# DeltaNet and a GELU block: copies of the queries' scores split over two engines, weight conversions placed later in a slot, one DMA moved to another queue

## The chip, the cores and the metric

The kernel runs on one core of a Trainium2 chip. The core has five engines with instruction queues of their own: PE (TensorE, matrix products), DVE (VectorE), ACT (ScalarE), POOL (GpSimd) and SP (SyncE), which here only issues DMAs. Each engine works through its queue in order; semaphores tie the queues together. The metric is the time of one execution in device microseconds; lower is better.

## What is computed

Four sequences (B) with eight heads (H), 768 tokens (S) and a head size of 48 (D) run through a recurrence with a delta rule; its output, laid out as 3072 rows of 384, runs through two dense layers with a quick GELU between them.

```python
k_n = k / (np.linalg.norm(k, axis=-1, keepdims=True) + 1e-06)
for t in range(S):
    y[:, :, t] = np.einsum('bhd,bhde->bhe', q[:, :, t], state)
    v_old = np.einsum('bhde,bhd->bhe', state, kt)
    state = state + bt[:, :, :, None] * np.einsum('bhd,bhe->bhde', kt, vt - v_old)
...
h = x @ w_in                             # 3072 x 384 by 384 x 2048
g = h * (1.0 / (1.0 + np.exp(-1.702 * h)))
return (g @ w_out).astype(np.float32)    # 2048 x 384
```

The attention inputs are float32. The weights w_in and w_out arrive as float64, so the kernel has to turn them into float32 itself.

## The kernel before

**Units.** The sequence is cut into 6 chunks of 128 tokens (C); a unit n is one chunk of one sequence with all its heads, 24 units, chunk by chunk (units 0 to 3 are chunk 0). Inside a chunk the recurrence is a triangular system in four blocks of 32 rows.

**Keys.** `prepare(n)` transposes the normalized keys (kT), multiplies them with themselves (psG), copies the products from PSUM to G (two copies; from unit 10 on the second is DVE's) and sends G to memory (Nd), from where the 32 x 32 diagonal blocks come back as NT with (head, block) on the partitions. `invert` inverts these blocks on DVE, for all four sequences at once in chunk 0 and for two at a time later (names NT, P, YB, YS); YS goes out to memory (Yd) and comes back as XB. In `prepare` both transfers of G are issued by SP: line 377 (Nd) and line 383 (NT).

**A unit's step.** `scores` transposes the queries (psT to QS) and forms their products with the keys (psQ); in chunks after the first the same product also holds a correction for V, which DVE subtracts at line 526. Line 527 copies the scores out of PSUM to M, four copies per unit, all on ACT; POOL then masks M (line 530). The substitution goes through the blocks 0 to 3: `solve` multiplies XB with V into psU, `solved` copies it to US on ACT, `below` multiplies G with it into psR, and `rest` subtracts psR from V on DVE. `outputs` gives psY, copied to xT and last; six small DMAs per pair of units move a part of last into xT (line 615).

**The dense layers.** `hidden` multiplies xT with w_in (ph, line 631) and applies the GELU on ACT (gT, line 636), `written` multiplies gT with w_out (po, line 646). They are generators; what is ready stands in `queue`.

**Weights.** There are 28 parts: 12 of w_in (128 x 512) and 16 of w_out (128 x 384). `fetch` loads the raw words of a part, three parts of w_in together for the first nine, mostly into places of w_out that are still unused; `from_double` turns a part into float32 with six to seven operations on DVE and, unless the part is among the first `NA`, one on ACT. `convert` also begins the next part. `ahead` fetches parts as long as their place is free. W0 parts are converted ahead of the first inversion, W1 after it, and `WB` gives the numbers for the first five slots.

**Slots.** `slot(n)` works on three units at a time in six groups: the later blocks of unit n - 1 (A), the blocks of unit n (B_), the start of unit n + 1 (D_). After each group it advances the inversion of a later chunk, converts weights (`more`, line 767) and takes dense work from `queue` up to a share of a cost. While the queue is empty, up to slot 2, it issues NB0 matmuls on constants instead (`warm`). Slots -1 to 1 are held in the order of the program (`in_order`, `pinned`); everywhere else the framework's scheduler sets the order on each engine. The records of helper calls in pinned stretches carry line 104.

Ahead of the slots, lines 804 to 831 set the order: fetch and convert one part, prepare units 0 to 3, load queries and values, scores of units 0 to 2, convert W0 - 1 parts, fetch ahead on SP's queue, `invert(0)`, normalize three more units, convert W1 parts.

Of the kernel before, what the change touches and what calls it, by code (L numbers as in the profile page):

```python
# [13 lines left out]
ACT = mybir.ActivationFunctionType  # L14
# [4 lines left out]
def kernel(  # L19
# [19 lines left out]
    nc = tc.nc  # L39

    B, H, S, D = q.shape
# [10 lines left out]
    HB = 2  # L52
    GR = 6
# [1 line left out]
    FQ = 4  # L55
    GB = 4

    W0, W1, WB = 2, 1, (2, 3, 5, 7, 8)
    NA = W0

    NW, NA0, NY, NB0 = 80, 3, 48, 3
    XR = DP - D
    NS = C * C + C
    assert S % C == 0 and H == 8 and D <= DP and DM == H * D == KC * 128
# [37 lines left out]
    def pinned(op):  # L102

        return lambda *a, **kw: tc.keep_in_program_order(op(*a, **kw))  # L104
# [13 lines left out]
    vec, act, pe = Engine(nc.vector), Engine(nc.scalar), Engine(nc.tensor)  # L118
# [184 lines left out]
    def normalize(n):  # L303
        K = KN[n % len(KN)][:, :, 0:D]
        mul = nc.gpsimd.tensor_tensor
        ksq = wk.tile([128, H, D], F32, tag="ksq", name="ksq", bufs=1)
        mul(ksq, K, K, op=ALU.mult)  # L307
        yield 0.0
        ssq = wk.tile([128, H], F32, tag="ssq", name="ssq", bufs=4)
        vec.tensor_reduce(ssq, ksq, axis=AX.X, op=ALU.add)  # L310
        rn = wk.tile([128, H], F32, tag="rn", name="rn", bufs=4)
        nc.gpsimd.tensor_tensor(rn, ssq, half, op=ALU.pow)  # L312
        yield 0.0
        vec.tensor_scalar(rn, rn, 1e-6, None, op0=ALU.add)
        vec.reciprocal(rn, rn)
        mul(K, K, rn.broadcast_to([128, H, D]), op=ALU.mult)
        yield 0.0
# [27 lines left out]
    def transposed(src, dst, early=False):  # L345

        pool_, tag = (ps_seq, "seq") if early else (ps_big, "big")
        psT = pool_.tile([128, NP, 128], F32, tag=tag, name="psT")
        flat = src.rearrange("p h d -> p (h d)")
        for j in range(NP):  # L350
            pe.transpose(psT[:, j, :], flat[:, j * 128 : (j + 1) * 128], ident)
        act.activation(dst, psT, ACT.Copy)  # L352

    def prepare(n):

        c, b = units[n]
        kn = KN[n % len(KN)]
        kT = wk.tile([128, NP, 128], F32, tag="kT", name="kT", bufs=6)
        transposed(kn, kT, c == 0)
        yield 0.6  # L360
        G = wk.tile([128, H, 128], F32, tag="G", name="G", bufs=6)
        pool_, tag = (ps_moe, "moe") if c == 0 and b % 2 else (ps_big, "big")
        ps = [pool_.tile([128, NP, 128], F32, tag=tag, name="psG") for _ in range(2)]
        for h in range(H):
            r = slice(h % 2 * 64, h % 2 * 64 + D)
            pe.matmul(  # L366
                ps[h % 2][:, h // 2], lhsT=kT[r, h // 2, :], rhs=kT[r, h // 2, :],
                start=True, stop=True,
            )
        act.activation(G[:, 0::2], ps[0], ACT.Copy)  # L370
        if n < 2 * B + HB:
            act.activation(G[:, 1::2], ps[1], ACT.Copy)
        else:
            vec.tensor_copy(G[:, 1::2], ps[1])

        Nd = dram.tile([H * NS], F32, tag="Nd", name="Nd", bufs=4)
        nc.sync.dma_start(
            out=Nd.rearrange("(h r) -> h r", r=NS)[:, 0 : C * C].rearrange(
                "h (p k) -> p h k", k=C
            ),  # L380
            in_=G,
        )
        nc.sync.dma_start(
            out=NT[b * NB * H : (b + 1) * NB * H],
            in_=Nd.rearrange("(d r) -> d r", r=NS // NB)[:, 0 : BS * C].rearrange(
                "d (i k) -> d i k", k=C
            )[:, :, 0:BS],
        )
        ready[n] = kn, kT, G
# [91 lines left out]
    class Step:  # L481
# [19 lines left out]
        def scores(self):  # L501

            c, S = self.c, slice(128, 128 + D)
            self.QS = wk.tile([128, NP, 128 + D], F32, tag="QS", name="QS", bufs=3)
            self.M = wk.tile([128, H, 128], F32, tag="M", name="M", bufs=3)
            transposed(self.qp, self.QS[:, :, 0:128])
            if c > 0:
                St = ST[:, self.b, 0 : NP * D].rearrange("p (j d) -> p j d", j=NP)
                act.activation(self.QS[:, :, S], St, ACT.Copy)
            yield  # L510
            n = 128 + D if c > 0 else 128
            for g in range(0, NP, 2):
                pool_, tag = (ps_seq, "seq") if g else (ps_big, "big")
                ps = [pool_.tile([128, 2, 128 + D], F32, tag=tag, name="psQ") for _ in range(2)]
                for i in range(2):
                    for hh in range(2):
                        r = self.rows(hh)
                        pe.matmul(  # L518
                            ps[hh][:, i, 0:n], lhsT=self.kT[r, g + i, :],
                            rhs=self.QS[r, g + i, 0:n], start=True, stop=True,  # L520
                        )
                for hh in range(2):
                    hs = slice(2 * g + hh, 2 * g + 4, 2)
                    if c > 0:
                        Vh = self.V[:, hs, :]
                        vec.tensor_tensor(Vh, Vh, ps[hh][:, :, S], op=ALU.subtract)  # L526
                    act.activation(self.M[:, hs, :], ps[hh][:, :, 0:128], ACT.Copy)  # L527
                if g == 0:
                    yield
            nc.gpsimd.affine_select(  # L530
                out=self.M, in_=self.M, compare_op=ALU.is_gt, fill=0.0, base=0,
                pattern=[[0, H], [1, 128]], channel_multiplier=-1,
            )
# [151 lines left out]
    def run(work):  # L685
        for _ in work:
            pass
# [38 lines left out]
    def slot(n, share):  # L726

        nonlocal inverting
        A, B_, D_ = steps.pop(n - 1, None), steps.get(n), None
        P = prepare(n + B) if B <= n + B < len(units) else iter(())
        m = n - 2 + len(KN)
        K = normalize(m) if len(KN) <= m < len(units) else iter(())
        left = WB[n + 1] if n + 1 < len(WB) else 0
        todo = share
        for group in range(GR):
            if group == 0:  # L740
                next(P, None)
                D_ = steps.get(n + 1) or new_step(n + 1)
                next(D_.scored, None)
            elif group == 1:
                together([(B_, 1)], [(A, 2)])
                next(D_.scored, None)
            elif group == 2:
                run(D_.scored)
            elif group == 3:
                together([(A, 3), (D_, 0)], [(B_, 1)])  # L750
                run(P)
            elif group == 4:
                if A:
                    A.queries()
                    A.outputs()
            else:
                together([(B_, 2)], [(D_, 0)])
                if A:
                    A.state()
            next(K, None)  # L760
            if group == GR - 1 and n % HB == 1:

                m = n + 1 + HB
                if B <= m < len(units):
                    inverting = invert(*units[m], HB)
            ahead_of(inverting, 5 if n % HB == 1 else 4)
            more = -(-left // (GR - group))
            run(weights(more))
            left -= more
            if queue and (n, group) != (HB, 0):  # L770
                for cost in take(todo / (GR - group)):
                    todo -= cost
            if not queue and n <= HB:
                warm(NB0)
        if n + 1 == len(WB) - 1:
            run(weights(n_parts))
        if n % HB == 0:
            run(inverting)
        if B <= n + B < len(units):
            load(n + B, ((QP, q),), sync if n < B else nc.sync.dma_start)  # L780
        if n > 0:
            m = n - 1 + len(KN)
            if m < len(units):
                load(m, ((KN, k),), sync if n < B else nc.sync.dma_start)
            if n - 1 + B < len(units):
                load_values(n - 1 + B)
            h = (n - 1) // HB
            if h == 0:
                i = (n - 1) % HB
                queue.append(hidden(xTs[h], gT0, slice(i * C, (i + 1) * C), 0.67))  # L790
            if n % HB == 0:
                gT = gT0 if h == 0 else []
                if h > 0:
                    queue.append(hidden(xTs[h], gT, slice(0, NTH), 1.3))
                queue.append(written(*units[h * HB], gT))
                xTs.pop(h)
# [70 lines left out]
```

## Time and profile before

The median of seven runs is 845.61 us (841.61 to 846.62). The profiled execution took 841.82 us.

| What | us |
|---|---|
| profiled execution, its span | 841.82, 840.1 |
| PE busy | 780.1 (93%) |
| DVE busy | 486.0 (58%) |
| ACT busy | 221.1 (26%) |
| POOL busy | 109.4 (13%) |
| ph (line 631) and po (line 646) on PE | 273.7 and 268.1 |
| M (line 527) on ACT, 96 copies | 33.0, 386 ns each |
| first multiplication of the inversion (NT) | starts at 31.92 |
| inversion's result YS done | 59.46 |
| first dense matmul (ph) | starts at 108.80 |

Busy time is the sum of an engine's instructions; PE's is to be read with care, since matmuls overlap and their ends are modelled. The page also cuts the span into 40 slices and gives for each the busy share of every engine in tenths, and the granted clock of TensorE. A row of the timeline gives the start, the duration, the engine (SPq, POOLq are DMA issues), the line, the operation with the names of output and inputs, the count, and in brackets the idle time of the engine before it and what ended it. The chain of waits follows the execution back from its last instruction, at each step to what released it.

### The profile page before, as it was taken

To read this page: it belongs to the slowest core of one execution; us is meant where nothing else is said; L and a number is where in the kernel's file an instruction comes from. 1 tells how busy PE (TensorE), PEld (TensorE's weight loads), DVE (VectorE), ACT (ScalarE), POOL (GpSimd) and SP (SyncE) were. 2 spreads that over 40 slices of the span, in tenths; PEclk is the share of its full clock that TensorE was granted. 3 is DMA by queue.
4 is the path that set the end of the run, shared out by engine and by line. 5 is a ranking of instruction groups with operands and counts; after the bars stand their busy time and mean duration, and the time that the engine had idled before them with its cause. 6 is when DMAs were issued, how large, how long until landed. Compare 5 with 4: busy or idle time off the path is not lost.

```text
span 840.1 us, 18659 instructions
## 1 busy us (share of the span) xinstructions
PE 780.1 (93%) x8040; PEld 572.6 (68%) x8040; DVE 486.0 (58%) x1065; ACT 221.1 (26%) x470; POOL 109.4 (13%) x128
## 2 busy tenths in 40 slices
PE   8337789979999999999999999999999999999998
PEld 7326678647767866867766767766767768677684
DVE  6798869987786493493592493592591771110000
ACT  3212534333322322322222322222223213211020
POOL 2013220132022102102102102102100000000000
PEclk9557679989999999999999999999999999999999
DMA  9969633723314213223222223223223020000000
GB/s 145 191 113 173 192 94 100 150 50 75 72 34 90 62 43 68 61 50 64 57 51 59 61 51 68 51 53 71 50 53 73 8 56 5 11 16 1 24 1 19
DMA packets 160977, 55.96 MB, mean 67 GB/s; under 512 B 128672, under 2 KB 157568, under 8 KB 160896
## 3 DMA queue, kind: packets, MB, share of 16 engines
q1 hardware_dynamic: 157760, 45.24, 26.4%
q0 software_dynamic: 2304, 9.44, 4.3%
q8 instruction: 63, 1.03, 0.5%
q10 hardware_dynamic: 832, 0.10, 0.1%
q14 instruction: 18, 0.15, 0.1%
HBM read 33.13 MB, written 20.45 MB: 64 GB/s over the span
## 4 chain that ended last, share of the span: by engine, by line
PE 61%; DVE 20%; DMA 7%; issue 5%; POOL 3%; SPq 2%; ACT 1%; DVEq 0%; POOLq 0%
PE ph L631 23%; PE po L646 21%; PE psU L550 4%; PE psY L566 4%; DVE P L408 3%; DMA KN<-in_k_dram 2%; PE psQ L518 2%; PE psG L366 2%; POOL rn L312 2%; DVE P L425 2%; DMA w_out<-in_moe_w_in_dram 2%; DVE P L104 2%; DVE YB L429 2%; PE ps_warm L153 2%; DVE YB L409 1%
## 5 line engine op out<-in xcount | busy, mean ns | idle before, releaser
L631 PE MATMUL ph<-xT,w_in 128*128 128x256 f32 (+1 forms) x1248 | 273.7, 372 | 11.3 <-ACT gT L636 8.3
L646 PE MATMUL po<-w_out,gT 128*128 128x384 f32 x768 | 268.1, 496 | 2.0 <-DVE w_out L193 2.0
L631 PEld LDWEIGHTS ph<-xT,w_in 128*128 128x128 f32 x1248 | 220.0, 193 | 49.7 <-ACT gT L636 10.7
L646 PEld LDWEIGHTS po<-w_out,gT 128*128 128x128 f32 x768 | 140.8, 190 | 91.4 <-issue 5.3
L546 DVE TENSOR_TENSOR V<-V,psR 32x384 f32<-32x384 f32 x87 | 48.4, 556 | 106.9 <-PE psR L539 105.1
L636 ACT ACTIVATE gT<-ph 128x512 f32<-128x512 f32 (+1 forms) x104 | 57.9, 566 | 165.0 <-PE ph L631 165.0
L557 ACT COPY US<-psU 32x384 f32<-32x384 f32 x88 | 41.3, 470 | 137.4 <-PE psR L539 118.9
L550 PEld LDWEIGHTS psU<-V,XB 32*32 32x32 f32 x1408 | 51.9, 107 | 31.0 <-issue 19.6
L550 PE MATMUL psU<-V,XB 32*32 32x48 f32 x1408 | 62.3, 207 | 1.7 <-DVE V L546 1.1
L530 POOL TENSOR_SCALAR_AFFINE_SELECT M<-M 128x1024 f32<-128x1024 f32 x24 | 27.5, 1144 | 268.4 <-ACT M L527 268.4
L539 PE MATMUL psR<-US,G 32*32 32x48 f32 x2080 | 60.2, 205 | 0.0
L527 ACT ACTIVATE M<-psQ 128x256 f32<-128x256 f32 x96 | 33.0, 386 | 89.6 <-DVE V L526 83.2
L653 DVE COPY o<-po 128x384 f32<-128x384 f32 x24 | 13.3, 554 | 74.3 <-PE po L646 74.1
L539 PEld LDWEIGHTS psR<-US,G 32*32 32x32 f32 x2080 | 50.4, 107 | 1.5 <-issue 1.4
L425 DVE TENSOR_TENSOR P<-NT,YB 64x2 f32<-64x2 f32 (+4 forms) x135 | 49.0, 363 | 4.1
L518 PE MATMUL psQ<-QS,kT 48*128 48x176 f32 (+1 forms) x384 | 44.0, 349 | 5.0 <-ACT QS L352 4.9
L429 DVE TENSOR_REDUCE YB<-P 64x2 f32<-64x2 f32 (+4 forms) x135 | 43.3, 321 | 4.1
L307 POOL TENSOR_TENSOR ksq<-KN 128x384 f32<-128x384 f32 x17 | 14.7, 866 | 234.6 <-DMA KN<-in_k_dram 234.6
L518 PEld LDWEIGHTS psQ<-QS,kT 48*128 48x128 f32 x384 | 31.9, 206 | 17.0 <-ACT QS L352 6.6
L607 DVE COPY last<-psY 128x128 f32<-128x128 f32 x20 | 5.8, 288 | 55.1 <-PE psY L566 55.0
L153 PE MATMUL ps_warm<-ident 128*128 128x256 bf16 x146 | 22.2, 320 | 15.8 <-DVE ps_warm L104 13.5
L408 DVE TENSOR_TENSOR P<-NT,YB 64x1024 f32<-64x1024 f32 (+3 forms) x36 | 31.7, 903 | 0.3
(116 smaller groups left out, 764.4 us busy)
## 6 DMA issues: line engine op xcount, KB each, us to landing
Nd<-G SPq DMA_DIRECT2D x24, 512.0 KB, 3.2
w_out<-in_moe_w_out_dram POOLq DMA_DIRECT2D x14, 384.0 KB, 3.9
KN<-in_k_dram SPq DMA_DIRECT2D x24, 192.0 KB, 3.2
QP<-in_q_dram SPq DMA_DIRECT2D x24, 192.0 KB, 3.6
V<-in_v_dram SPq DMA_DIRECT2D x24, 192.0 KB, 3.1
out_dram<-o SPq DMA_DIRECT2D x24, 192.0 KB, 2.0
NT<-Nd SPq DMA_DIRECT2D x24, 128.0 KB, 2.7
Yd<-YS SPq DMA_DIRECT2D x24, 128.0 KB, 2.2
```

Source lines behind the costliest of these rows:

```text
L153: pe.matmul(ps, lhsT=ones[:, 0:128], rhs=ones, start=True, stop=True)
L408: tt(P, a, b, op=ALU.mult)
L425: tt(P, diag(Nf, i * BS, [[0, i], [1, i]]), diag(Yf, 0, [[BS, i], [1, i]]), op=ALU.mult,)
L429: red(diag(Yf, i, [[BS, i]]), P, axis=AX.X, op=ALU.add, negate=True)
L518: pe.matmul(ps[hh][:, i, 0:n], lhsT=self.kT[r, g + i, :], rhs=self.QS[r, g + i, 0:n], start=True, stop=True,)
L539: pe.matmul(psR[u, h, :], lhsT=self.G[r, h, u], rhs=self.U[r, h, :], start=True, stop=True,)
L546: vec.tensor_tensor(self.V[u], self.V[u], psR[u], op=ALU.subtract)
L550: pe.matmul(psU[r, h, :], lhsT=inverse[self.n][r, h, :], rhs=self.V[r, h, :], start=True, stop=True,)
L557: act.copy(self.U[r], psU[r])
L631: pe.matmul(ph[:, u], lhsT=w_in[:, j, f * 128 : (f + 1) * 128], rhs=xT[:, j, t], start=(j == 0), stop=(j == KC - 1),)
L636: act.activation(gT[f0 // FQ][:, f0 % FQ : f0 % FQ + 2, t], ph, ACT.Gelu_apprx_sigmoid)
L646: pe.matmul(po, lhsT=gT[f // FQ][:, f % FQ, i * C : (i + 1) * C], rhs=w_out[:, f, :], start=(f == 0), stop=(f == FC - 1),)
```

## The change

Five things differ. (1) W0 goes from 2 to 3, and WB's first entry from 2 to 1: one more part is converted ahead of the first inversion and one fewer in slot -1; the sum stays 28. As NA is W0, that part is converted on DVE alone. The place of the first group is then free earlier, so `ahead(2, sync)` fetches two groups on SP's queue rather than one. (2) NB0 goes from 3 to 6. (3) For chunk 0 the DMA from G to Nd is issued by ACT. (4) From unit 10 on, two of the four copies to M are DVE's; the others are written as act.copy. (5) The number of parts per group is rounded down rather than up, so they fall into a slot's last groups: of three parts, for instance, groups 3 to 5 get one each, before it was groups 0 to 2.

```diff
-    W0, W1, WB = 2, 1, (2, 3, 5, 7, 8)
+    W0, W1, WB = 3, 1, (1, 3, 5, 7, 8)
     NA = W0
 
-    NW, NA0, NY, NB0 = 80, 3, 48, 3
+    NW, NA0, NY, NB0 = 80, 3, 48, 6
...
         Nd = dram.tile([H * NS], F32, tag="Nd", name="Nd", bufs=4)
-        nc.sync.dma_start(
+        dma = pinned(nc.scalar.dma_start) if c == 0 else nc.sync.dma_start
+        dma(
...
                         vec.tensor_tensor(Vh, Vh, ps[hh][:, :, S], op=ALU.subtract)
-                    act.activation(self.M[:, hs, :], ps[hh][:, :, 0:128], ACT.Copy)
+                    copy = act.copy if hh == 0 or self.n < 2 * B + HB else vec.tensor_copy
+                    copy(self.M[:, hs, :], ps[hh][:, :, 0:128])
...
             ahead_of(inverting, 5 if n % HB == 1 else 4)
-            more = -(-left // (GR - group))
+            more = left // (GR - group)
             run(weights(more))
             left -= more
```

## The prediction

> **What bounds the kernel now.** I read the slices of the page first, then a table by stages, then the waits, and last the chain of waits in one steady stretch.
>
> ```profile
> PE   8337789979999999999999999999999999999998
> DVE  6798869987786493493592493592591771110000
> PEclk9557679989999999999999999999999999999999
> DMA  9969633723314213223222223223223020000000
> ```
>
> Each digit is a slice of 21 us. PE (TensorE) is thin only in the first five or six slices. There DVE (VectorE) and the DMA engines are full, and TensorE's clock is halved. From slice 10 on PE shows 9 to the end. So a gain must come from the first 200 us, or from the small waits that PE still has later.
>
> ```profile
> 59.00:80.00 21.00, 16.47 (x174) 12.58 (x175) 17.55 (x44) 4.31 (x7) 6.86 (x12) 0.74 1.00 165
> 80.00:102.00 22.00, 19.71 (x361) 15.29 (x355) 19.24 (x37) 10.10 (x20) 5.26 (x10) 0.54 0.64 166
> 102.00:115.00 13.00, 7.92 (x119) 6.84 (x118) 8.55 (x20) 6.10 (x12) 2.50 (x5) 0.70 0.64 191
> ```
>
> The columns are the stretch, its length, then PE, weight loads, DVE, ACT, POOL busy, the clock, DMA share, GB/s. Up to 102 us DVE is the full engine: it converts the float64 weights between the steps of the substitution. The places where it, or PE behind it, stands still are in the timeline:
>
> ```profile
> 24.01 1.64 SPq L377 DMA_DIRECT2D Nd<-G  x2
> 31.92 1.23 DVE L104 TENSOR_TENSOR NT<-NT,bI 128x1024 f32<-128x1024 f32 x1 [5.17 <-DMA NT<-Nd]
> 77.90 0.43 DVE L104 TENSOR_SCALAR w_in<-w_out 128x512 int32<-128x512 int32 x1 [2.58 <-DMA w_out<-in_moe_w_in_dram]
> 108.80 1.20 PE L631 MATMUL ph<-xT,w_in 128*128 128x128 f32 x4 [2.94 <-DMA xT<-last]
> ```
>
> The brackets give the idle time before the row and what ended it. DVE idles 5.17 us ahead of the first inversion, then 2.58 us for a weight group. The dense stage (ph, po) starts only when the first xT has landed, at 108.80. In the steady part the chain of waits shows a loop that recurs every pair of slots (about 61.5 us):
>
> ```profile
> 445.79 3.06 DMA KN<-in_k_dram
> 448.92 0.84 POOL ksq L307
> 449.78 0.56 DVE ssq L310
> 450.41 1.65 POOL rn L312
> 452.28 0.57 DVE V L546
> 453.11 0.59 DVE V L526 x3
> 453.73 0.38 ACT M L527
> 454.11 0.50 ACT gT L636
> 454.65 5.84 PE ph L631 x18
> ```
>
> Read downward: the keys land late, VectorE's in-order queue waits for their norm, so V, the copy M and the activation gT are late, and PE waits 1.65 us for gT. Six such waits sum to 8.1 us. The loop has a PE leg (gT to the next key load, some 15 us) and a DVE leg (the inversion, 46 us), in series.
>
> **A. Third part ahead of the substitution, and the loads it frees.** In the 7.69 us from 19.05 to 26.74 DVE converts two parts and two operations (0.42 and 0.69) of the third, so a part alone costs (7.69 - 1.11)/2 = 3.29. Three take 9.9 and end at 28.9, inside the idle stretch before 31.92. What leaves the path after the inversion is the rest of that part, L190, L191, L193: 0.42 + 0.68 + 0.69 = 1.8 us. Its cover ends if NT lands before 28.9. The four loads of the third weight group (parts 6 to 8, 2 x 576 + 2 x 192 KB = 1.5 MB), issued by POOL at 62.10 and landing at 77.8, now go on SP's queue right behind the second group. The DMA engines stood at 0.02 from 54 to 60; at the 150 GB/s of the second group 1.5 MB take 10.2 us, so they land near 63. The 2.58 us wait goes. Queued behind them on SP are Yd and XB, the way back of the inversion, which landed at 61.5 and 64.0. In the built program the XB loads wait for the same semaphores as the third group; I put them near 67. The cover is PE's warm matmuls, which ran to 66.8 and now run to about 67. Cost 0 (0 to 3).
>
> **B. Chunk 0's scores on ScalarE's queue.** The third Nd left at 24.01 though its G was ready at 22.1, the fourth at 24.6 instead of 23.0: SP was held by the NT loads ahead of them. On ACT they leave after the copies, plus about 0.6 us of ACT time for each issue (the beta loads: 2.61 us for four), about 22.6 and 23.8. The Trainium skill ("DMA: Bandwidth & Descriptors", Issuing engines are not separate DMA queues) speaks against more: transfers from several engines share the same 16 DMA engines, and only issue time is saved. By the held issues the gain would be up to 1.6; by the rule, with the engines 0.75 to 1.07 busy here, near nothing. I take 0.9 (0 to 2).
>
> **C. Conversions late in a slot, 6 warm matmuls for 3.** A part in the slots costs DVE 2.73 us (80.97 to 83.69). Between the first update of V and the one that releases unit 0's outputs (V at 92.42), the order of before has parts 5 to 8, the changed order 5 to 7. The walk: inversion ends at 58.6 (0.9 earlier); normalizing takes the 9.19 us of before (59.46 to 68.65) less the 1.79 of A and 0.39 of the part begun in it, 7.0, to 65.6; parts 3 and 4, 5.45, to 71.0; two V, 1.14, to 72.2. Then DVE has only one small operation until PE and ACT bring the next V: psU 1.5, US 0.5, solves 1.7, and 12 warm matmuls at 0.13 to 0.24 each, with the latencies 6 us, to 78.2 (up to 80.5). Parts 5 and 6, two V, part 7, one V (5.46 + 1.14 + 2.73 + 0.56) end at 88.1, against 92.98. That is 4.9 earlier, A and B included.
> The 60 added warm matmuls lie in PE's waits, except the three ahead of psY: 0.82 becomes 1.46, cost 0.64. What they do to the clock: it fell to 0.50 after PE idled from 68.4 to 72.7. "TensorE: Matmul & The Clock Gate" (Part 1) says an idle window of about 3.4 us halves the rate and as much steady work restores it. The walk leaves PE idle for about 4 us again while DVE does parts 5 and 6, so by row and rule the outputs still run at half rate; with a held clock psG, warm and psY would save 2 us. I take the half rate.
> So xT is issued 4.2 us earlier, at 96.4. Now three instead of two of its six loads stand behind NT, which waits for Nd; I keep the 8.0 us from issue to landing and put the start of the dense stage at 104.5. Two things I let cancel: in the changed order PE has solves, psG and psQ ahead of the first ph, which fill the 2.94 us, but one w_out part (2.0 us of DVE) is left for later. Bounds for the stage: -9 (4.2, the 2.9 filled, 2 of clock) and +5 (rival 3).
>
> **D. M copied by two engines.** From unit 10 on, 28 copies of 128x256 go to DVE. No such row exists there; between its PSUM copies 128x128 (0.288) and 128x384 (0.554) I take 0.42. ACT loses 28 x 0.386, which it had idle. Two lie in each DVE leg, which is full: +0.84; four legs end in a wait of PE, 3.4 us. In the PE leg gT no longer stands behind the second M, -0.27 (the spacing of those rows) in five loops; and in four of these the built order has V L546 ahead of the norm, so the first psQ subtraction comes at 452.28, not 453.11: -0.83. Sum 3.4 - 1.35 - 3.3 = -1.3; ends -4.7 (the legs cost nothing) and +4.2 (all five count, the order brings nothing). Of units below 10 only the name of the copy changes: 0.371 for such a COPY against 0.386.
>
> **Sum.** -4.2 - 1.3 = -5.5 on the profiled execution's 841.82 (span 840.1), so 836.3. That run belongs to the lower of the seven times; the median, 845.61, lies 3.8 above. On its scale I forecast 840.1. Faster by over 0.3% means below 843.1, about what a measurement can tell from no change.
>
> **Rivals**, on the same scale.
> 1. The start is earlier, but the last w_out parts are not. POOL fetches them one behind another as places come free (158.52, 160.20, 165.54, 175.01), 3.9 us each to land, and po waits at 182.23 for a conversion. If that chain stays put, only D is left: 844.3. For it: one part more is left for later. Against: in the built order po stands behind more solves.
> 2. All works: start -4.2, the 2.94 us filled, and no wait at 182, after which the clock fell to 0.74 in 180 to 200 (some 2 us): with D -10.4, 835.2. For it: the rows; against: DVE is 98% busy from 130 to 160 and may not follow.
> 3. Slower: the late conversions starve DVE. The first round already leaves it 5.6 us without work, since its parts stand behind the next update; a round at half clock costs 6 to 8. If the three further rounds before 105 us leave it 3 us each, 9 us are added to the forecast's -5.5: +3.5, 849.1. It decides once new idle time of DVE in slots 0 and 1 passes 5.5 us. Against: parts 5 to 11 stand between those updates in the built order, 2.73 us each.
>
> **Chances.** Forecast (own range 837 to 843) 0.46, rival 1 0.18, rival 2 0.19, rival 3 0.17. Faster 0.65, same 0.18, slower 0.17. The range 834 to 849 leaves out the far tails of rivals 2 and 3, and half of the latter.
>
> **What would show it.** Right: NT's multiplication at 31.0 or before with conversions ahead of it until 29; no DMA wait of DVE near 78; V for unit 0's outputs near 88; first ph at 104.5; PE's waits for gT near 1.4 (the first) and 1.3 (the others). Wrong: XB landing after 68, a DVE gap over 8 us near 74, xT landing after 107, a po wait over 3 us near 180, or waits for gT over 2.5 us.

## The result and the profile after

The changed kernel takes 834.27 us, median of 12 runs (828.16 to 841.72); the kernel before, run beside it, 843.22. The ratio is 0.9895 (95% interval 0.9875 to 0.9915): 8.9 us less (7.2 to 10.5). One of the twelve executions, 841.72 us, fell in a slower state and is left out of the ratio. The profiled execution took 833.18 us (span 831.2), against 841.82 (840.1).

The slices of the page, as they were read before:

```profile
PE   8438799899999999999999999999999999999998
DVE  6898899778984593493593592692692871110000
PEclk9559989969999999999999999999999999999999
DMA  9996732732323223223223224124123020000000
```

In slices 4 to 6 the clock is 9, 9, 8 where it was 7, 6, 7, and the DMA engines, at 6 in the third slice before (42 to 63 us), are at 9 there: the third weight group has moved into it. The table by stages shows the same, with the columns as before (length, PE, weight loads, DVE, ACT, POOL, clock, DMA share, GB/s):

```profile
59.00:80.00 21.00, 20.41 (x326) 16.64 (x325) 17.38 (x43) 5.82 (x11) 5.52 (x10) 0.92 0.66 138
80.00:102.00 22.00, 14.50 (x293) 11.87 (x293) 19.74 (x38) 11.55 (x24) 5.12 (x10) 0.95 0.78 187
102.00:115.00 13.00, 13.00 (x160) 12.08 (x154) 10.45 (x31) 5.97 (x13) 5.13 (x4) 0.68 0.55 138
```

Between 80 and 102 us the granted clock is 0.95 where it was 0.54, and between 102 and 115 PE is busy throughout, where it had 7.92 us of work before, though at a clock of 0.68. The timeline has these rows at the places shown before:

```profile
22.11 0.37 ACTq L104 DMA_DIRECT2D Nd<-G  x1
23.15 0.41 ACTq L104 DMA_DIRECT2D Nd<-G  x1
31.00 1.22 DVE L104 TENSOR_TENSOR NT<-NT,bI 128x1024 f32<-128x1024 f32 x1 [1.31 <-DMA NT<-Nd]
...
96.68 0.36 DVE L181 TENSOR_SCALAR w_out<-w_out 128x384 int32<-128x384 int32 x1 [1.62 <-DMA w_out<-in_moe_w_out_dram]
99.49 2.15 PE L366 MATMUL psG<-kT 48*128 48x128 f32 x16 [2.42 <-ACT M L529]
103.73 1.22 DVE L104 TENSOR_TENSOR NT<-NT,bI 64x1024 f32<-64x1024 f32 x1
104.78 1.22 PE L633 MATMUL ph<-xT,w_in 128*128 128x128 f32 x4
```

The last two scores leave at 22.11 and 23.15; DVE idles 1.31 us ahead of the first inversion, not 5.17; no row near 78 waits for a weight group any more. The first ph stands at 104.78 and waits for nothing. The second inversion (NT, 64 partitions) begins at 103.73, before ph; in the kernel before, it began at 112.08, after it. Two waits are longer or new: DVE stands 1.62 us for a w_out part at 96.68 (0.53 before), and PE 2.42 us behind ACT's copies to M, which come after that part's operations in ACT's queue; with PE's wait the clock falls to 0.50. Last the chain of waits in one steady stretch (start, duration, what):

```profile
440.53 4.53 DMA KN<-in_k_dram
...
445.13 0.84 POOL ksq L307
...
445.99 0.56 DVE ssq L310
...
446.63 1.65 POOL rn L312
...
449.11 0.61 ACT gT L638
...
449.76 4.15 PE ph L633 x18
```

The loop is still there: late keys, their norm, gT, PE. How far the changed kernel is ahead at four markers of the two profiled executions:

| Marker | before | after | ahead |
|---|---|---|---|
| V for unit 0's outputs done | 92.98 | 86.76 | 6.2 |
| first ph | 108.80 | 104.78 | 4.0 |
| wait for gT near 325 ends | 331.30 | 325.34 | 6.0 |
| wait for gT near 571 ends | 580.13 | 571.45 | 8.7 |

So some two thirds of it stand at 325 us, and the rest comes in the steady loops.

### The profile page after: what moved, and what is told of

The parts are those of the page before. It is cut to its first block, busy times and chain, and to the rows that moved or that the text cites. A ratio compares the mean times of both kernels' runs of the same rounds, so it can differ in the third digit from the quotient of the medians.

```text
span 831.2 us, 18809 instructions
## 1 busy us (share of the span) xinstructions
PE 776.4 (93%) x8100; PEld 571.8 (69%) x8100; DVE 494.5 (59%) x1095; ACT 212.7 (26%) x441; POOL 105.8 (13%) x124
## 3 DMA queue, kind: packets, MB, share of 16 engines
q8 instruction: 63, 1.03, 0.5%
## 4 chain that ended last, share of the span: by engine, by line
PE 65%; DVE 19%; DMA 7%; POOL 3%; issue 2%; SPq 2%; ACT 1%; DVEq 0%; POOLq 0%; ACTq 0%
PE ph L633 26%; PE po L648 21%; PE psU L552 4%; PE psY L568 4%; DMA KN<-in_k_dram 3%; DVE P L426 3%; PE psQ L519 3%; PE psG L366 3%; DVE P L409 2%; DVE YB L430 2%; POOL rn L312 2%; DVE P L104 2%; PE psR L541 2%; PE ps_warm L153 2%; SPq L617 1%
## 5 line engine op out<-in xcount | busy, mean ns | idle before, releaser
L648 PEld LDWEIGHTS po<-w_out,gT 128*128 128x128 f32 x768 | 140.7, 190 | 93.8 <-issue 5.1
L548 DVE TENSOR_TENSOR V<-V,psR 32x384 f32<-32x384 f32 x87 | 48.4, 556 | 95.0 <-PE psR L541 93.3
L529 ACT COPY M<-psQ 128x256 f32<-128x256 f32 x68 | 24.2, 375 | 79.7 <-DVE V L527 75.1
L153 PEld LDWEIGHTS <-ident 128*128 128x128 bf16 x152 | 17.2, 115 | 20.6 <-issue 13.9
```

What stands on the lines that cost most here:

```text
L153: pe.matmul(ps, lhsT=ones[:, 0:128], rhs=ones, start=True, stop=True)
L548: vec.tensor_tensor(self.V[u], self.V[u], psR[u], op=ALU.subtract)
L648: pe.matmul(po, lhsT=gT[f // FQ][:, f % FQ, i * C : (i + 1) * C], rhs=w_out[:, f, :], start=(f == 0), stop=(f == FC - 1),)
```

## The experiments

Twelve kernels. In experiments 1 to 6 one edit of the change is undone or varied, in 7 single edits are made alone, in 8 an edit that the change doesn't have. Ratios are to the kernel before on the same chip. Two executions of one kernel differ by several us with the granted clock (last section). In two profiles of the changed kernel (the one above and e5) the first ph lies 0.8 us apart and the wait near 571 1.5, so I take a single place in a profile as good to about 1 us early on and 3 us later.

**1. The warm matmuls (e1): NB0 back to 3.**

```diff
-    NW, NA0, NY, NB0 = 80, 3, 48, 6
+    NW, NA0, NY, NB0 = 80, 3, 48, 3
```

> The changed kernel with NB0 back at 3; all else as changed. The record's step C (the 60 more warm matmuls cost 0.64 us and leave the clock at half rate while unit 0's outputs run): the granted clock between 80 and 102 us is the same with 3 as with 6, and the time is 0 to 0.6 us below the changed kernel. The clock theory (the trace of the changed kernel shows 0.95 there, before 0.54): with 3 the clock falls to about 0.55 again, psG, psY and the first ph come 2 us or more later, and the time is 2 to 3 us above the changed kernel. A third theory: the clock falls, but DVE's conversions set the pace there, so that the time changes by less than 0.5 us.

Measured: ratio 0.9894 (0.9867 to 0.9922), as the changed kernel's 0.9895; the two intervals together leave about 3 us either way. The stage of this kernel, columns as above:

```profile
80.00:102.00 22.00, 16.95 (x322) 13.54 (x318) 18.81 (x36) 11.20 (x23) 4.80 (x10) 0.73 0.69 188
```

The clock does fall, from 0.95 to 0.73, and the first ph comes at 106.92, 2.1 us later. But at the wait for gT near 571 this profile is only 0.2 us behind (571.69), mostly since its waits for gT between 320 and 590 sum to 4.5 us, not 5.8. How much of the clock is the warm matmuls' is less sure than 0.95 against 0.73 makes it look: the changed kernel's second profile (e5) has 0.84 there. That the edit brings 2 us in the end isn't shown.

**2. The copies to M (e2): all four on ACT.**

```diff
-                    copy = act.copy if hh == 0 or self.n < 2 * B + HB else vec.tensor_copy
+                    copy = act.copy
```

> The changed kernel with all four copies to M on ACT (act.copy); all else as changed. The record's step D: the two copies on DVE bring 1.3 us, so without them the time is 1.3 us above the changed kernel and the five waits for gT are longer by about 0.3 each. The traces of before and after lie 6.0 us apart at the wait near 325 us and 8.7 us apart at the one near 571 us: by that, 2.7 us belong to the steady part, and all of it should go here (2.7 us above the changed kernel, gT waits of 1.6 again in the last two loops). If the copies cost DVE's legs as much as they bring, no difference beyond 0.5 us.

Measured: 0.9959 (0.9929 to 0.9988), so 3.5 us faster than before where the change is 8.9. That 3.5 averages two groups of executions: seven take 833.9 to 836.6 us, five 840.9 to 844.0 at a lower mean clock. The profiled one, 833.89, is of the first group, so the edit's worth is best read from its stages. Its five waits for gT sum to 8.6 us (1.86, 1.18, 2.63, 1.15, 1.76) against 5.8. From the first to the last of them it takes 249.3 us, the changed kernel 246.1: D is worth 3.2 us there.

**3. Chunk 0's scores (e3): sent by SP again.**

```diff
-        dma = pinned(nc.scalar.dma_start) if c == 0 else nc.sync.dma_start
+        dma = nc.sync.dma_start
```

> The changed kernel with chunk 0's Nd sent by SP again. The record's step B: NT's multiplication starts 0.9 us later (31.9 instead of 31.0), conversions still hide the wait, and the time is 0.9 us above the changed kernel. The rule of the page (shared DMA engines, only issue time saved): below 0.3 us. Third: later slack takes the 0.9 us up, NT at 31.9 but the first ph within 0.3 us of its place.

Measured: 0.9919 (0.9895 to 0.9944), 6.8 us faster than before, or 2.1 us less gain than the change, with some 2.7 us of uncertainty. In the profile YS and V come 0.8 us later (V for unit 0's outputs done at 87.58), as step B has it, but the first ph at 104.57 doesn't. The inversion's gain is shown by all the profiles together: NT's multiplication starts at 30.3 to 31.0 where ACT sends the scores (nine profiles), at 31.2 to 31.9 where SP does (five). What of it reaches the end is open.

**4. Late conversions (e4): rounded up again.**

```diff
-            more = left // (GR - group)
+            more = -(-left // (GR - group))
```

> The changed kernel with the parts per group rounded up again (early in a slot). The record's step C: of the 4.9 us by which V for unit 0's outputs comes earlier, 2.7 are A and B, so 2.2 us are this edit: V for these outputs at about 88.9 us instead of 86.2 to 86.8, the time 2 us above the changed kernel. If the 3 us idle of DVE that late parts leave cost what they bring: within 0.5 us. If the early parts also hold the first V back as they did before (74.2 instead of 71.2) and the clock falls with PE's longer wait: 4 to 6 us above.

Measured: 0.9973 (0.9954 to 0.9992): only 2.3 us faster than before. This one edit carries 6.6 us of the change, give or take 2.3. V for unit 0's outputs ends at 88.94, 2.2 us later, just as step C has it; but that is not what decides, since the first ph (104.53) is not later at all. DVE's timeline in this kernel:

```profile
103.53 0.36 DVE L104 TENSOR_TENSOR ST<-psS,ST 128x192 f32<-128x192 f32 x1
108.79 0.56 DVE L548 TENSOR_TENSOR V<-V,psR 32x384 f32<-32x384 f32 x1 [4.91 <-PE psR L541]
109.38 1.22 DVE L104 TENSOR_TENSOR NT<-NT,bI 64x1024 f32<-64x1024 f32 x1
```

And PE's in the same kernel:

```profile
104.53 1.20 PE L633 MATMUL ph<-xT,w_in 128*128 128x128 f32 x4 [2.13 <-DMA xT<-last]
105.65 1.65 PE L366 MATMUL psG<-kT 48*128 48x128 f32 x8
107.23 0.28 PE L552 MATMUL psU<-V,XB 32*32 32x48 f32 x1
```

PE waits for xT with the first ph at the head of its queue, and the solve that V L548 needs stands behind it. DVE's pinned order has the second inversion behind that V, so DVE idles 4.91 us and the inversion begins at 109.38. In the changed kernel the solve stands ahead of ph (psU from 101.57), DVE idles 0.67 us there, and NT is at 103.73: 5.65 us earlier. The kernel before had the same stall, 4.12 us ahead of V L546 at 111.49. What follows goes with the second inversion, not with the first ph. The wait for gT near 325 ends at 320.9 to 327.1 in the seven profiles that have it and begin that inversion at 102.7 to 105.4 (the first ph of e1 and e9, two of them, stands at 106.92 and 106.07), and at 329.4 to 332.5 in the three that begin it at 109.4 to 112.1, e4 with its ph at 104.53 among them. (e7, 108.28 and 338.69, has a low clock in between.) At that wait e4 is 4.1 us behind the changed kernel; what it loses after it can't be parted from the clock, which falls twice there (0.94 in 380 to 410 and in 440 to 470).

**5. The first edit (e7): W0 = 2 again, with the changed kernel once more on the same chip (e5).**

```diff
-    W0, W1, WB = 3, 1, (1, 3, 5, 7, 8)
+    W0, W1, WB = 2, 1, (2, 3, 5, 7, 8)
```

> The changed kernel itself, unchanged, so that the undone parts have it on the same chip. All theories: 8 to 10 us below the kernel before; waits for gT in the steady part between 0.4 and 2 us. By the clock theory of the steady part, a run in which a wait for gT is followed by a stretch of half clock (a window of 30 us at 0.94) is 1.7 us longer for each such stretch, so that time and granted clock go together over the runs.

> The changed kernel with W0 = 2 and WB = (2, 3, 5, 7, 8) again: the third part is converted after the inversion, and its group is fetched later by POOL. The record's step A: 1.8 us of conversion back after the inversion, so YS at the same place but the normalization and the first V 1.8 us later (73.5 instead of 71.7), and DVE waits for the third group at about 77 again if that part stands there: 1.8 to 4 us above the changed kernel. Theory of the cover: as with Nd (e3: V 0.8 us later, the first ph in place), the later waits take it up, below 1 us.

Measured: e5 0.9908 (0.9875 to 0.9940), median 835.54; e7 0.9940 (0.9916 to 0.9965), median 838.37. So A is worth about 2.8 us, with intervals that overlap. Its mechanism is not the one that was expected of e7: the first V comes earlier (70.07), not later, and the loss is the wait for the third group.

```profile
78.03 0.43 DVE L104 TENSOR_SCALAR w_in<-w_out 128x512 int32<-128x512 int32 x1 [3.11 <-DMA w_out<-in_moe_w_in_dram]
...
88.86 0.56 DVE L104 TENSOR_TENSOR V<-V,psR 32x384 f32<-32x384 f32 x1 [0.72 <-PE psR L104]
```

V for unit 0's outputs ends at 89.42, 2.7 us after the changed kernel's, and the first ph, for which PE waits 4.91 us, stands at 109.04, 4.3 later. (The profiled execution of e7 was the longest of its runs, 845.24 us, with a low clock from 130 us on; only rows ahead of that are used here.)

**6. The early group (e10): the third part converted early, only one group on SP's queue.**

```diff
-    ahead(2, sync)
+    ahead(1, sync)
     run(invert(0))
```

> The changed kernel with the third part still converted in front of the inversion, but only one group fetched ahead on SP (ahead(1, sync)), so that POOL fetches the third group; DVE's order is the same. It parts the two halves of step A. If the conversion in the idle stretch is what pays (1.8 us): within 0.5 us of the changed kernel. If the early group pays (the DMA wait of 2.58 us before, 3.1 us in e7): DVE waits for the group near 73 to 78, and the time is 2 to 3 us above the changed kernel. XB, then no longer behind the group on SP, should land at 64 instead of 67.4.

Measured: 0.9871 (0.9845 to 0.9898), at least as fast as the change. It didn't part what it was to part: with its place free, POOL issued the group at 29.96, still earlier than SP would have, and DVE had no wait for it. Nor does XB come earlier: POOL's group delayed SP's loads, so that the second group left SP only at 51.34, right ahead of Yd. Yd was issued at 57.73 and the XB loads, which wait for it, at 65.09, 7.4 us later. In the kernel before, that took 2.0 us (59.49 to 61.47), with the DMA engines at 0.00 from 56 to 60; in the changed kernel they stand at 1.03 from 56 to 60, and it takes 6.2 us (58.45 to 64.70). One weight group in front of Yd costs as much as two; whether by SP's queue or by the engines' load isn't parted.

**7. Single edits on the kernel before: M alone (e6), late conversions alone (e9).** The diffs are edits (4) and (5) of the change.

> The kernel before with edit (4) alone: from unit 10 on two of the four copies to M are DVE's. The record's step D: 1.3 us faster (range 4.7 faster to 4.2 slower), waits for gT near 1.3. By the traces of before and after: 2.7 us faster, with the last two waits at 0.5. By the changed kernel without it (e2, medians 3 to 5 us above): 4 us faster. If the copies only help together with the other edits: within 1 us.

> The kernel before with edit (5) alone: parts per group rounded down, late in a slot. The record's step C: 2.2 of the 4.9 us by which V for unit 0's outputs comes earlier belong to it (90.8 instead of 92.4 to 93.0), 2 us faster than before. By the changed kernel without it (e4, 5 to 6 us above the changed kernel): 5 us faster. Theory that late parts pay only once the third group is there (in the changed kernel without the early group, e7, DVE waits 3.1 us for it at 78): DVE waits for the group near 75 with nothing else to do, and the time is within 1 us of before, or up to 3.5 us above it, as rival 3 has it.

Measured: e6 0.9954 (0.9935 to 0.9974), 3.9 us faster. Its steady part, from the wait near 332 to the one near 578, takes 245.96 us against 248.83: 2.9 us. e9 0.9925 (0.9897 to 0.9953), 6.3 us faster, by itself two thirds of the whole gain. DVE in e9:

```profile
75.77 0.56 DVE L104 TENSOR_TENSOR V<-V,psR 64x384 f32<-64x384 f32 x1 [0.93 <-PE psR L104]
77.83 0.43 DVE L104 TENSOR_SCALAR w_in<-w_out 128x512 int32<-128x512 int32 x1 [1.50 <-DMA w_out<-in_moe_w_in_dram]
83.41 1.14 DVE L104 TENSOR_TENSOR V<-V,psR 32x384 f32<-32x384 f32 x2
87.40 0.56 DVE L104 TENSOR_TENSOR V<-V,psR 32x384 f32<-32x384 f32 x1
```

Rival 3 finds no support: the late parts leave DVE 2.4 us idle between the first V and the one for unit 0's outputs, where the kernel before had 4.2 (2.58 for the group, 1.65 for psR). V for unit 0's outputs ends at 87.96, 5.0 us earlier by this edit alone, and the second inversion begins at 103.20. Undone alone, A costs 2.7 us at that V and late conversions 2.2; done alone, late conversions bring 5.0 of the 6.2. The two edits take away the same stalls, so their single values don't add: undone one at a time, the five edits lose some 17 us by the ratios, twice the gain.

**8. Keys sent by ACT: on the changed kernel (e8), with M on ACT (e11), on the kernel before (e12).**

```diff
-                load(m, ((KN, k),), sync if n < B else nc.sync.dma_start)
+                load(m, ((KN, k),), sync if n < B else nc.scalar.dma_start)
```

> The changed kernel with the key loads of the steady part (KN, slots from 4 on) issued by ACT instead of SP, where they stand behind six xT and two Yd DMAs (435.7 to 440.5 in the changed kernel). If the late keys set the waits for gT, as the chain of waits shows (KN, ksq, ssq, rn, V, M, gT): KN leaves some 5 us earlier, the five waits (5.8 us in sum) go nearly to zero, 3 to 6 us below the changed kernel. If DVE's inversion leg is what sets the loop, the waits stay: within 1 us. If ACT's queue holds the load behind gT, or the load holds gT up: slower, by up to 2 us for each slot pair.

> The faster kernel of e8 (keys sent by ACT) with all four copies to M on ACT again. If D brings its 2.7 to 3.2 us only by shortening the wait for gT, which the earlier keys have removed: within 1 us of e8 (823 to 825). If it shortens DVE's or ACT's legs in themselves: 2.5 to 3.5 us above e8. If the two copies now cost DVE more than they bring: 1 to 3 us below e8.

> The kernel before with one edit that is not part of the change: the key loads of the steady part issued by ACT. If SP's order is what couples the loop's two legs, in the kernel before as in the changed one: all five waits for gT (7.9 us) go, 8 to 11 us faster than before, near 832, as much as the whole change brings, and no stretch of half clock is left between 320 and 590 us. If the loop is bound by DVE's inversion: within 2 us of before.

Measured: e8 0.9756 (0.9730 to 0.9781), median 823.74 us: 20.6 us below the kernel before and about 12 below the change, more than was expected. It is the fastest kernel here and beats both. e12 0.9891 (0.9868 to 0.9914): this one edit on the kernel before brings as much as all five of the change. The timeline of e8 in the loop shown above:

```profile
428.79 0.38 ACTq L89 DMA_DIRECT2D KN<-in_k_dram  x1
...
434.02 0.54 DVE L310 TENSOR_REDUCE ssq<-ksq 128x8 f32<-128x384 f32 x1
434.64 1.64 POOL L312 TENSOR_TENSOR rn<-ssq,half 128x8 f32<-128x8 f32 x1 [1.41 <-DVE ssq L310]
434.94 0.98 SPq L465 DMA_DIRECT2D Yd<-YS  x2
```

The keys leave as soon as psS has read the old ones. Now SP's queue of the changed kernel, with the row that reads the old keys (psS) and the copy to `last`:

```profile
432.56 0.67 PE L590 MATMUL psS<-US,KN 128*64 128x48 f32 x16
...
435.29 0.29 DVE L609 COPY last<-psY 128x128 f32<-128x128 f32 x1
...
435.66 3.67 SPq L617 DMA_DIRECT2D xT<-last  x6
439.43 0.99 SPq L465 DMA_DIRECT2D Yd<-YS  x2
440.53 0.39 SPq L89 DMA_DIRECT2D KN<-in_k_dram  x1
```

There they stand behind six xT, which wait for DVE's `last` (a copy that DVE makes between operations of the inversion), and two Yd, which carry the inversion's result. Of the 7.3 us from psS's end at 433.2 to the keys' issue at 440.53, 2.4 are the wait for `last`, and 4.9 are the eight DMAs, issued one after another. That order in one queue is what ties the two legs of the loop together. With the keys on ACT no wait of PE for gT over 0.3 us is left after 130 us, and PE's busy time between 320 and 590 us, of 270, in the kernel before, the changed kernel and e8:

```profile
320.00:590.00 270.00, 261.94 (x2817) 190.72 (x2815) 152.25 (x332) 70.60 (x152) 39.43 (x36) 0.99 0.28 61
```

```profile
320.00:590.00 270.00, 263.58 (x2899) 193.04 (x2898) 159.69 (x363) 67.02 (x138) 39.36 (x36) 1.00 0.27 59
```

```profile
320.00:590.00 270.00, 269.60 (x2961) 197.77 (x2960) 162.17 (x371) 70.19 (x141) 39.92 (x36) 1.00 0.26 59
```

So 6.0 of the 7.7 us between the spans of the last two profiles lie in this stretch; that their medians differ by some 12 comes with the spread of executions (e8's profiled one, 825.51, is among its slowest).

e11 has 0.9798 (0.9774 to 0.9822), median 824.38 on another chip; its profiled span is 822.0, e8's 823.5. Whether the split of M still brings anything once the waits are gone stays open: the ratios say some 3.5 us, with intervals that just overlap, the profiled executions say no.

## Why the prediction was right, and where its sum was short

The forecast was 5.5 us faster (836.3 on the profiled execution's scale); the profiled execution gave 8.6 (833.18), the ratio 8.9. The direction and the wide range held; the forecast's own range did not: on its scale the ratio gives 845.61 x 0.9895 = 836.7, just below 837. The step that was mis-sized most is the dense stage in C: the start was put at 4.2 us in all, and it brought 6.0 by 325 us. In part it was luck that the sum came as near as it did, since errors of both signs met in it. Step by step:

- **What bounds it**: right. The gain came from the start (6.0 of 8.7 us stand at 325 us) and from the small waits for gT.
- **A**: the conversions end at 29.69 (28.9 forecast), NT's multiplication stands at 31.00, and the DVE wait of 2.58 us is gone. XB: psU began at 67.44, forecast 67; the cover held. Whether A pays by the group or by the conversion in the gap stays open: e7 loses it by the DVE wait of 3.11 us, and e10, meant to part the two, had the group early as well.
- **B**: 0.9 at NT, as forecast (31.92 to 31.00; 22.11 and 23.15 for the issues, forecast 22.6 and 23.8). What was saved is the time that the scores stood behind the NT loads on SP; the prediction's reading of the rule on issuing engines, that this comes to near nothing while the DMA engines are busy, was too strict. That all of it reaches the end was assumed; e3 neither shows nor excludes it.
- **C, V for unit 0's outputs**: 88.1 forecast, 86.76 measured. The walk was right for the first V (72.29 against 72.2). From there on the waits were shorter: the next update of V stood at 76.04 after 2.70 us idle, not at 78.2; psU, costed 1.5 at half rate, took 0.86. The clock that stays "at half rate" was wrong. From 68 to 72 us PE was idle but for 0.38 us before and is busy for 4.00 now, for two reasons. One is the added warm matmuls. The other, which the walk missed, is ACT's queue, before (first two rows) and after:

```profile
71.62 0.72 ACT L104 ACTIVATE w_in<-w_in,low 128x512 int32<-128x512 int32 x1 [1.88 <-DVE w_in L104]
72.25 0.45 ACT L104 COPY US<-psU 32x384 f32<-32x384 f32 x1
...
68.34 0.47 ACT L104 COPY US<-psU 32x384 f32<-32x384 f32 x1 [0.31 <-PE psU L104]
```

Early parts put ACT's share of a conversion, which waits for DVE, ahead of the copy to US that PE needs; late parts don't. In e9, by that edit alone, PE waits 0.47 us there, not 4.38. The one wait of 4 us that the walk had for PE during parts 5 and 6 came as waits of 1.64 and 1.72, with work between them, and the clock stayed at 1.00 until 100 us. The Trainium skill's rule ("TensorE: Matmul & The Clock Gate", Part 1), which asks for an idle window of about 3.4 us, is not enough to foretell this: the clock of the changed kernel fell at 100 us after a wait of 2.42, in e9 it fell near 72 after one of 1.40, and in e5, the same kernel as changed with waits of 1.65 and 1.73, it fell at 89. By e1 the warm matmuls show in the stage, and not clearly in the time.

- **C, the dense stage**: here the sum failed. The start of ph was right (104.5 forecast, 104.78), but by luck: xT was issued at 94.61, not 96.4, and ph no longer waits for it, since PE, at half clock from 100 us, still has psG, the solve and psQ to do. And I took it as the only marker of the stage, and wrote that the 2.94 us wait, filled by solves, and the w_out part left for later "cancel". They don't. With the solve ahead of ph the second inversion starts 8.35 us earlier (112.08 to 103.73), DVE loses its 4.12 us stall, and near 325 us the kernel is 6.0 us ahead, not 4.2. e4 shows it from the other side: with V only 2.2 us later but the stall back, 6.6 us are lost in the end, 4.1 of them by the wait near 325.
- **D**: 1.3 forecast; 2.7 between the gT markers of before and after, 3.2 by e2, 2.9 by e6. The copy took 415 ns (420 forecast). The term that was off is "+0.84 per DVE leg". From each NT to the YS that follows, four legs sum to 139.9 us in before and 140.7 in e6, and to 141.9 in e2 and 143.0 in the changed kernel: the copies cost 0.8 and 1.1 us, not 3.4. Not because the copies are cheap: from the start of each to the start of the next instruction the eight take 3.1 us. The inversion gives it back. Before (first two rows), and in e6:

```profile
365.60 1.09 POOL L530 TENSOR_SCALAR_AFFINE_SELECT M<-M 128x1024 f32<-128x1024 f32 x1 [10.88 <-ACT M L527]
366.05 2.04 DVE L408 TENSOR_TENSOR P<-NT,YB 64x768 f32<-64x768 f32 x2
...
366.15 0.41 DVE L528 COPY M<-psQ 128x256 f32<-128x256 f32 x1
366.69 1.09 POOL L531 TENSOR_SCALAR_AFFINE_SELECT M<-M 128x1024 f32<-128x1024 f32 x1 [10.51 <-DVE M L528]
367.61 1.58 DVE L408 TENSOR_TENSOR P<-NT,YB 64x768 f32<-64x768 f32 x2
```

With all of M on ACT, DVE's 64x768 multiplication starts 0.45 to 0.58 us into POOL's mask of M and takes 1.32 to 1.44 us by itself (the rows hold it and the next one); with two copies on DVE the mask is nearly over by then, and it takes 0.95 to 0.98. So it is in all sixteen legs of the four kernels, 1.6 to 1.7 us for four legs. (In e6 one leg gains another 0.4 at a smaller multiplication beside POOL.) Of the changed kernel's 3.1 this leaves 1.5, of which 1.1 was measured; the last 0.4 isn't resolved. No experiment moved the mask alone. The five legs from YS to NT gain 2.4 (e6) and 3.8 (e2), less than the 4.65 forecast; so the two errors partly offset.

**The rivals.** Rival 1 (w_out chain stays put) is out: po's first matmul moved from 151.75 to 145.33. Its waits for w_out even grew, to 3.5 us at 166 and 171, and took the place of others: part of rival 2's bonus was given back so. Rival 2 (10.4 us) is nearer to 8.9 than the forecast of 5.5, and right in what it added first, the filled wait; the waits for w_out near 182, which it had gone, moved forward instead. Rival 3 is contradicted by e9.

## What to carry to other kernels

Look for the in-order queue in which the thing that is late stands behind things that wait for something else or take long to issue: PE with ph ahead of a solve, ACT with a conversion ahead of US, SP with xT and Yd ahead of the keys. To move one such item is worth more than shortening the work (e12: one word, 9 us). When an instruction is added to a "full" leg, ask also what it shifts: here the copies were paid in full, and half came back where a multiplication no longer met POOL's mask. And judge a stage by each engine that leaves it, not by the first matmul of the next one.

## What the runs showed of the hardware

**Time goes with the granted clock, within one kernel.** Two executions of the changed kernel took 828.16 us at a mean clock of 0.970 and 838.44 at 0.953; 10.3 us for 0.017. In the steady part, stretches of 30 us at 0.94 lie where PE has waited for gT (2.63 us in e2, 1.65 in the kernel before at 454.65, where the 18 matmuls after it take 5.84 us, not 4.15), but not wherever it has: of e3's two waits of 2.10 us one has such a stretch and one has not. So a small wait of PE has a price beyond its own length, but not every time.

**A short write to memory behind a weight group takes three times as long** as with idle DMA engines (Yd's issue to XB's: 2.0 us in before, 6.2 in the changed kernel, 7.4 in e10; Yd's own landing: 2.2, 6.1 and 7.2). In the changed kernel the warm matmuls hid it but for 0.28 us; in e10 PE waited 2.0.

**A DVE multiplication that starts under a POOL operation takes longer**: 1.32 to 1.44 us against 0.95 to 0.98 for the 64x768 form beside the mask of M.
